# Masked attention with a rational FFN on one core: 64-row score products, sums in PSUM, loads on one queue, a new order

## The chip, the core and the metric

The kernel runs on one core of a Trainium2 chip. The metric is device time in microseconds, the median of several runs. Before the change it is 1323.82 us (three runs, 1321.93 to 1325.02).

## The reference

```python
def _attn_ref(q, k, v, tau):                      # q, k, v: 8 x 8 heads x 576 x 64, f32
    scores = matmul(q, k^T) / sqrt(64)
    thresh = max(scores, axis=-1) - tau
    scores = where(scores >= thresh, scores, -1e9)
    attn = exp(scores - max(scores))
    attn = attn / (sum(attn) + 1e-9)
    return matmul(attn, v)

def _moe_ref(x, w_in, w_out, a, b):               # x: 4608 x 512; w_in 512 x 2048; w_out 2048 x 512
    h = x @ w_in
    P = a[0] + a[1]*h + a[2]*h**2 + a[3]*h**3
    Q = 1 + |b[0]|*|h| + |b[1]|*h**2
    return (P / (Q + 1e-6)) @ w_out
```

The attention's output, heads side by side, is the x of the second function. Only scores within tau of their row's maximum survive.

## The kernel before

**Attention units.** The 64 heads are worked in 32 pairs, `bp`, four pairs to each of 8 batches. A head pair's queries lie in one buffer `QQ`, head 0 in partitions 0 to 63 and head 1 in 64 to 127 (the contracted dimension is 64); its keys lie likewise in `KK`. There are two buffers of each (`NQ = 2`). A pair has four *full* units, 128 queries of both heads, and one *rest* unit, the last 64 queries (`REM`) of both heads put on 128 PSUM partitions: 160 units in all. A unit makes 128 x 576 scores per head (one such tile for a rest unit).

One unit goes through these steps (functions in `unit_ops`):

- `f_qk` (L760 for rest units, L769 and L773 for full ones): the score products on TensorE. A full unit has two 64-row products of 512 keys, one per head, and one 128-row product for the last 64 keys of both, with zeros laid in `KK` so that the heads don't mix. A rest unit has two 128-row products, again with zeros in `QQ`. They write three PSUM banks, 0 to 2 (or 3 to 5, taken in turns, in the first 21 units, `SINGLE`). Head 0 lies at the start of bank 0 and runs 64 columns into bank 1; head 1 ends at the end of bank 2 and begins in the last 64 columns of bank 1. The middle of bank 1 is unused.
- `f_max` (L779, L781) on VectorE, then `f_thr` (L786, L788) on either of ScalarE and VectorE.
- `f_pre` (L794) on ScalarE reads the scores from PSUM and leaves the masked ones in an SBUF buffer `e`; after it the banks are free for the next unit.
- `f_sum` (L798) on ScalarE: the exponential, in place in `e`, with its row sum written by the accumulator (a second instruction, ACTIVATION_READ_ACCUMULATOR) to a small SBUF tile `st`.
- `f_rec`, `f_rec2` (L803 or L805, L809): one over the sum.
- `f_hi`, `f_lo` (L303, L305, L820): the weights as two f16 parts; `f_tp` (L830): two DMA transposes from SyncE's queue; `f_av` (L889): the products with v, as column-split products on halves of the array; `f_xh`, `f_xl` (L899, L905): the result as two f16 parts, the FFN's x. In the first batch the transposes are products with a diagonal matrix instead (L843, L848, L873).

**FFN steps** (`moe_ops`): groups of four 128-row slices of the hidden layer for 256 tokens: `f_g1` (L1006, 128-row f16 products), `f_h` (L1015), the rational function on VectorE and ScalarE (L1020 to L1048), a split in two parts (L295, L297, L1056) and `f_g2` (L1065, f32r products). Weights are decoded from f64 words at the start. The last three token chunks are left for the time after the attention.

**Loads.** `load_ops` loads the queries (`ldq`, L614 to L616) and the keys (`ldk`, L621 to L626) of a pair, twice per pair for three of a batch's four pairs, 56 visits in all. Queries take three DMAs, keys three to five. For the first eight pairs they go out on SyncE (keys of the first two pairs on ScalarE's queue), for the others on GpSimd's queue. There they stand with the loads of v, of the weights and with the output stores. A load waits for a free buffer, and everything behind it on its queue waits with it.

**What sets the order.** Each of these steps is entered with `op(engine, duration, key, ...)` in a planner, `Plan`. It goes through all steps, gives each engine whichever of its ready steps can start first by the planner's durations (ties within `TOL` go to the smaller key), assigns banks and buffers, and calls the steps' functions in the order of planned starts. That order is the program's; at run time each engine goes through its own list in order, with semaphores between. Steps that can run on either of two engines (`FLEX`) are weighed by `EARLY` and `PRICE`. Where TensorE would idle before 400 us, filler products are put in (`f_warm`, L1205). `plan.rank` is the unit's place, which also sets who gets buffers first.

Of the kernel before, what the change touches and what calls it, by code (L numbers as in the profile page):

```python
# [8 lines left out]
F32 = mybir.dt.float32  # L9
# [28 lines left out]
SINGLE = 21  # L38
# [7 lines left out]
NQ = 2  # L46
# [15 lines left out]
UP = 2.0 ** -14  # L62
TPD = 1.3

AHEAD_RANK = 2.3359
# [9 lines left out]
        "ev": {"ACT": 0.465, "DVE": 0.6}, "ev1": {"ACT": 0.156, "DVE": 0.196}, "A": {"ACT": 0.583, "DVE": 0.341},  # L75
        "gh": {"ACT": 0.52, "DVE": 0.33}, "wh": {"ACT": 0.57, "DVE": 0.38}}

EARLY = {"ACT": 1.2758, "DVE": 3.4372}
EARLY_END = 714.5248
PRICE = {"ACT": 1.064, "DVE": 2.2723}  # L80

TOL = {"PE": 0, "ACT": 0.129, "DVE": 0.1, "POOL": 0.1, "DMA": 0, "GD": 0}
WARM, WARM_END = 0.6, 400.0
# [24 lines left out]
class Plan:  # L108
# [7 lines left out]
    def __init__(self):  # L116
        self.ops, self.pools = [], {}
        self.warm = None
        self.banks = [0.0] * 8
        self.rank = 0.0  # L120

    def pool(self, name, n):
        self.pools[name] = [(0.0, i) for i in range(n)]
# [1 line left out]
    def op(self, eng, dur, key, fn, after=(), take=(), drop=()):  # L125
        engs = {eng: dur} if isinstance(eng, str) else eng
        o = Op(engs, key, fn, [x for x in after if x is not None], list(take), list(drop))
        o.rank = self.rank
        self.ops.append(o)
        return o  # L130

# [122 lines left out]
def masked_attention_rational_ffn(  # L254
# [83 lines left out]
    ones = bass.AP(one.tensor, one.offset, [list(one.ap[0]), [0, P]])  # L338


    QW = S + REM
    QQs = [const.tile([P, QW], F32, name=f"QQ{i}") for i in range(NQ)]
    KKs = [const.tile([P, QW + REM], F32, name=f"KK{i}") for i in range(NQ)]
    for t in QQs:
        nc.gpsimd.memset(t[:, NT * P:], 0.0)
    for t in KKs:
        nc.gpsimd.memset(t[0:D, S:QW], 0.0)
        nc.gpsimd.memset(t[D:P, 0:REM], 0.0)
# [40 lines left out]
    def scale_ops(key, get, up, inv, s, after, ahead=0.0):  # L389


        box = {}
        plan.rank = key - ahead
# [12 lines left out]
        def f_all():  # L406
            box["all"] = bank(hb)[:, 0:P]
            nc.tensor.matmul(box["all"], ones, box["d"], start=True, stop=True)

        def f3():  # L410
            p2 = box["p2"]
            nc.vector.tensor_reduce(box["m2"], box["all"], AX.X, ALU.max)
# [32 lines left out]
    def decode_ops(i, key, load, hold, dst=None):  # L445


        box = {}
        plan.rank = key - AHEAD_RANK
        ht = Hold("u", 1)  # L450

        def ld():
            if not loaded:

                for x in KKs[0][:, REM:REM + 1], QQs[0][:, 0:1]:
# [146 lines left out]
    def load_ops(bp, ts):  # L602
        bb, pr = divmod(bp, NP)
        p = pos[(bp, ts[0])]
        plan.rank = p - 3.0
# [4 lines left out]
        queue, eng = (nc.sync, "DMA") if bp < EARLY_BP else (nc.gpsimd, "GD")  # L610

        def ldq():
            QQ = QQs[qh.slot]
            queue.dma_start(QQ[0:D, 0:S], qT[bb, pr, :, 0:S])  # L614
            queue.dma_start(QQ[D:P, 0:NT * P], qT[bb, pr, :, S + REM:])
            queue.dma_start(QQ[D:P, S:], qT[bb, pr, :, S:S + REM])  # L616

        def ldk():
            KK = KKs[kh.slot]
            kq_ = nc.scalar if bp < FROM_ACT else queue  # L620
            kq_.dma_start(KK[0:D, REM:S], kT[bb, pr, :, 0:NT * P])  # L621
            kq_.dma_start(KK[D:P, REM:QW], kT[bb, pr, :, S + REM:])
            kq_.dma_start(KK[0:D, 0:REM], kT[bb, pr, :, NT * P:S])
            if NT in ts:
                for i in range(2):
                    kq_.dma_start(KK[i * D:(i + 1) * D, QW:], kT[bb, pr, :, NT * P + i * REM:S + i * REM])  # L626

        q_done[bp] = [op(eng, 4.3 if first else 1.6, p0, ldq, (), [qh])]
        k_done[bp] = [op(eng, 0.1 if bp < FROM_ACT else 1.6, p0 + 0.1, ldk, (), [kh])]

    def is_plain(bp, t):

# [10 lines left out]

    def load_v_ops(bp):
        bb, pr = divmod(bp, NP)
        plan.rank = pos[(bb * NP, 0)]
# [79 lines left out]

    def unit_ops(bp, t):
        bb, pr = divmod(bp, NP)
        plan.rank = p = pos[(bp, t)]
        full = t < NT  # L730
        single = units.index((bp, t)) < SINGLE
        heads = (0, 1) if full else (0,)
        kh, qh = kq[bp]
        plain = is_plain(bp, t)
# [15 lines left out]
        def f_qk():  # L750
            QQ, KK = QQs[qh.slot], KKs[kh.slot]
            h = sh[0]
            s = ps[:, h.bank[0]:h.bank[-1] + 1, :].rearrange("p b k -> p (b k)")
            w = len(h.bank) * 512
            one = dict(start=True, stop=True)
            if not full:

                s = box["s"][0] = s[:, 0:S]
                for k0, c0, n in (REM, 0, NT * P), (QW, NT * P, REM):
                    nc.tensor.matmul(s[:, c0:c0 + n], QQ[:, NT * P:QW], KK[:, k0:k0 + n], **one)  # L760
                return

            box["s"][0], box["s"][1] = s[:, 0:S], s[:, w - S:]
            box["both"] = bass.AP(s.tensor, s.offset, [list(s.ap[0]), [w - S, 2], [1, S]])
            for hh in range(2):

                r = slice(hh * D, (hh + 1) * D)
                d = s[:, 0:NT * P] if hh == 0 else s[:, w - NT * P:]
                nc.tensor.matmul(d, QQ[r, t * P:(t + 1) * P], KK[r, REM:S], **one)  # L769

            dst, src = (bass.AP(x.tensor, x.offset, [list(x.ap[0]), [n, 2], [1, REM]])
                        for x, n in ((s[:, NT * P:S], w - 2 * NT * P - REM), (KK[:, 0:REM], S)))
            nc.tensor.matmul(dst, QQ[:, t * P:(t + 1) * P], src, **one)  # L773
# [16 lines left out]
        def f_pre(hh):  # L790
# [2 lines left out]
                box["e"] = place(e_hold)  # L793
            nc.scalar.activation(ev(hh), box["s"][hh], AF.Prelu, scale=SCALE, bias=box["st"][:, 2 + hh:3 + hh], alpha=STEEP)  # L794

        def f_sum(hh):
            e = box["e"][:, hh * S:(hh + 1) * S]
            nc.scalar.activation(e, e, AF.Exp, scale=passes, accum_out=box["st"][:, 4 + hh:5 + hh])  # L798

        def f_rec():  # L800
            r = box["st"][:, 6:6 + nh]
            if plan.eng == "ACT":
                nc.scalar.activation(r, box["st"][:, 4:4 + nh], AF.Copy, scale=UP, bias=1e-9 * UP)  # L803
            else:
                nc.vector.tensor_scalar(r, box["st"][:, 4:4 + nh], 1e-9, UP, ALU.add, ALU.mult)  # L805

        def f_rec2():
            r = box["st"][:, 6:6 + nh]
# [103 lines left out]
        qk = op("PE", 1.47 if full else 1.12, p, f_qk, need, [sh[0]], [kh, qh] * nh)  # L912
        if full:
            mx = op("DVE", 1.255, p + 0.1, lambda: f_max(None), [qk], [st_hold])
        else:
# [3 lines left out]
            ex[hh] = op("ACT", 0.63, p + 0.2 + 0.02 * hh, lambda hh=hh: f_pre(hh),  # L919
                        [thr[hh]] + ([ex[0]] if hh else []), [e_hold] if hh == 0 else (), [sh[hh]])  # L920
        for hh in heads:
            mk[hh] = op("ACT", 0.76, p + 0.3 + 0.02 * hh, lambda hh=hh: f_sum(hh), [ex[hh]])
# [51 lines left out]
    def moe_ops(ck, f0, nb, p, begins, ends, soon):  # L974
# [2 lines left out]
        kind, bb, half = ck  # L977
        late = p >= end
        g = f0 // NC
        plan.rank = p = max(p, w_key(g, 2 * NC) - 1.0, ranks[-1] + 0.01)  # L980
        ranks.append(p)
        name = f"{kind}{bb}_{half}_{f0}"
        FW = nb * CT
# [264 lines left out]
```

## Time and profile before

| | before |
|---|---|
| median of three runs | 1323.82 us (1321.93 to 1325.02) |
| span of the profiled execution | 1321.7 us |
| its granted TensorE clock, mean | 0.987 |
| TensorE busy | 1258.0 us (95%) |
| VectorE busy | 1218.1 us (92%) |
| ScalarE busy | 1118.6 us (85%) |
| GpSimd busy | 241.0 us (18%) |
| DMA moved | 146.67 MB, mean 111 GB/s |

The span, from first to last instruction of the profiled execution, is the only time given of that execution; it is 2.1 us under the median of the runs. In the rows PE is TensorE's products, PEld its weight loads, DVE VectorE, ACT ScalarE, POOL GpSimd, SP SyncE; a letter q behind an engine means its queue. A group's row gives line, engine, operation, operands, shapes and count, then total busy time and mean ns of one, then the idle time of the engine just before these instructions and what ended it. Ends of products are modelled, so lengths of single products overlap their successors, and starts are the safer reading.

### The profile page before, as it was taken

Reading aid. Unit: us, or ns where it says so; the run is one execution under the profiler, and the core shown is the slowest. Engines: PE = TensorE matmul, PEld = TensorE weight load, DVE = VectorE, ACT = ScalarE, POOL = GpSimd, SP = SyncE. Lnnn points to the kernel's source line nnn. Section 1 sums busy time; section 2 is a strip of 40 time slices with the busy share of each in tenths; the row PEclk is TensorE's granted clock in tenths of the full one; section 3 lists DMA queues with packets and bytes.
Section 4 is the critical chain, followed back from the end, with each engine's and each line's share of the span. In section 5 each row is a group of like instructions: output and inputs, shape, how many; then the busy total and the mean of one; then the engine's idle time right before and its main releaser. Section 6 shows DMA issues by size and latency. Waiting matters only on the chain. (4 is left out here: it accounts for less than half of the span.)

```text
span 1321.7 us, 25463 instructions
## 1 busy us (share of the span) xinstructions
PE 1258.0 (95%) x9476; PEld 936.0 (71%) x9476; DVE 1218.1 (92%) x1913; ACT 1118.6 (85%) x2182; POOL 241.0 (18%) x462
## 2 busy tenths in 40 slices
PE   7987998999999999999999899998999999999998
PEld 5665776777777767676677677766677777678886
DVE  4988999999999999998999899988999999998777
ACT  4998888899999989998999789877988899885564
POOL 2101000022312321322212231223212330200000
PEclk8999999999999999999999999999999999999999
DMA  7434373576767756665665584586765864641000
GB/s 203 130 101 140 106 152 73 99 137 129 144 115 119 150 104 121 118 138 117 117 97 105 94 155 102 126 116 118 127 104 108 144 146 81 134 82 37 17 17 16
DMA packets 340588, 146.67 MB, mean 111 GB/s; under 512 B 316208, under 2 KB 323184, under 8 KB 340464
## 3 DMA queue, kind: packets, MB, share of 16 engines
q1 hardware_dynamic: 316400, 86.49, 38.4%
q0 software_dynamic: 22784, 57.31, 15.9%
q10 hardware_dynamic: 1280, 1.25, 0.4%
q8 instruction: 75, 1.23, 0.4%
q14 instruction: 49, 0.40, 0.1%
HBM read 60.30 MB, written 9.44 MB: 53 GB/s over the span
## 5 line engine op out<-in xcount | busy, mean ns | idle before, releaser
L1065 PE MATMUL banks<-wp,g 128*128 128x512 f32 x1728 | 438.9, 403 | 3.9 <-DVE g L1056 3.0
L1006 PEld LDWEIGHTS <-wi 128*128 128x128 f16 x3456 | 332.7, 98 | 71.6 <-issue 33.5
L1006 PE MATMUL banks<-x,wi 128*128 128x256 f16 x3072 | 361.3, 274 | 14.5 <-ACT t L1015 13.3
L1065 PEld LDWEIGHTS banks<-wp,g 128*128 128x128 f32 x1728 | 315.3, 189 | 77.5 <-DVE g L1056 5.8
L798 ACT ACTIVATE e<-e,cf 128x576 f32<-128x576 f32 x288 | 221.5, 775 | 0.3
L303 ACT ACTIVATE hi<-e,st 128x576 f16<-128x576 f32 x229 | 174.0, 768 | 51.9 <-DVE st L809 40.1
L794 ACT ACTIVATE e<-banks,st 128x576 f32<-128x576 f32 x288 | 205.1, 735 | 11.0 <-DMA KK<-in_kT_dram 6.0
L820 DVE SCALAR_TENSOR_TENSOR e<-e,st,hi 128x576 f16<-128x576 f32 x252 | 204.1, 810 | 9.0 <-ACT hi L303 7.2
L779 DVE TENSOR_REDUCE st<-banks 128x2 f32<-128x1152 f32 x128 | 172.1, 1344 | 14.2 <-PE banks L773 13.9
L769 PE MATMUL banks<-KK,QQ 64*128 64x512 f32 x512 | 154.8, 652 | 9.1 <-DMA KK<-in_kT_dram 5.3
L889 PE MATMUL banks<-pT,V 128*64 128x256 f16 (+1 forms) x2520 | 125.2, 253 | 14.0 <-DMA pT<-e 9.3
L889 PEld LDWEIGHTS <-V 128*64 128x64 f16 x2520 | 107.4, 113 | 33.3 <-issue 24.2
L1015 ACT ACTIVATE t<-banks,hsc 128x512 f32<-128x512 f32 (+1 forms) x192 | 106.2, 575 | 24.2 <-PE banks L1006 19.0
L1042 DVE SCALAR_TENSOR_TENSOR t<-t,co,t 128x1024 f32<-128x1024 f32 (+1 forms) x73 | 92.1, 1262 | 18.9 <-ACT t L1036 18.9
L773 PEld LDWEIGHTS banks<-KK,QQ 128*128 128x128 f32 x256 | 38.6, 190 | 99.3 <-issue 88.7
L1033 ACT ACTIVATE t<-t,co 128x1024 f32<-128x1024 f32 (+1 forms) x73 | 82.7, 1133 | 29.8 <-DVE t L1039 29.3
L614 POOL DMA_DIRECT2D QQ<-in_qT_dram x42 | 22.1, 527 | 413.8 <-PE banks L760 248.0
L1056 DVE TENSOR_TENSOR g<-t,g 128x512 fp32r<-128x512 f32 x144 | 94.5, 682 | 2.6 <-ACT g L295 2.5
L1048 DVE SCALAR_TENSOR_TENSOR t<-t,co,t 128x1024 f32<-128x1024 f32 (+1 forms) x73 | 92.2, 1263 | 0.8
L1026 DVE SCALAR_TENSOR_TENSOR t<-t,co 128x1024 f32<-128x1024 f32 (+1 forms) x73 | 92.0, 1261 | 0.4 <-ACT t L1015 0.4
L1039 DVE SCALAR_TENSOR_TENSOR t<-t,co,t 128x1024 f32<-128x1024 f32 (+1 forms) x73 | 92.0, 1260 | 0.0
L1029 DVE SCALAR_TENSOR_TENSOR t<-t,co 128x1024 f32<-128x1024 f32 (+1 forms) x73 | 92.0, 1260 | 0.0
(130 smaller groups left out, 1540.7 us busy)
## 6 DMA issues: line engine op xcount, KB each, us to landing
t<-in_w_in_dram POOLq DMA_DIRECT2D x16, 512.0 KB, 5.1
t<-in_w_out_dram POOLq DMA_DIRECT2D x16, 512.0 KB, 4.9
out_dram<-u POOLq DMA_DIRECT2D x26, 256.0 KB, 3.0
V<-in_v_dram POOLq DMA_DIRECT2D x24, 256.0 KB, 4.6
QQ<-in_qT_dram POOLq DMA_DIRECT2D x42, 144.0 KB, 2.8
KK<-in_kT_dram POOLq DMA_DIRECT2D x42, 144.0 KB, 3.3
QQ<-in_qT_dram POOLq DMA_DIRECT2D x42, 128.0 KB, 2.7
KK<-in_kT_dram POOLq DMA_DIRECT2D x42, 128.0 KB, 2.7
```

The lines of the kernel that those rows point to most:

```text
L303: nc.scalar.activation(dst, src, AF.Identity, scale=factor)
L769: nc.tensor.matmul(d, QQ[r, t * P:(t + 1) * P], KK[r, REM:S], **one)
L779: nc.vector.tensor_reduce(box["st"][:, 0:2], box["both"], AX.X, ALU.max, negate=True)
L794: nc.scalar.activation(ev(hh), box["s"][hh], AF.Prelu, scale=SCALE, bias=box["st"][:, 2 + hh:3 + hh], alpha=STEEP)
L798: nc.scalar.activation(e, e, AF.Exp, scale=passes, accum_out=box["st"][:, 4 + hh:5 + hh])
L820: nc.vector.scalar_tensor_tensor(box["lo"][:, c], ev(hh), box["st"][:, 6 + hh:7 + hh], box["hi"][:, c], ALU.mult, ALU.subtract)
L889: nc.tensor.matmul(dst, V[:, c * P + hh * D:c * P + (hh + 1) * D], rhs, start=c == 0 and n == 0, stop=c == NT and n == 2)
L1006: nc.tensor.matmul(d, wi_tile(c, f0 + j, hl), x[:, c, :], start=c == 0 and n == 0, stop=c == NC - 1 and n == 2)
L1015: nc.scalar.activation(box["h3"][:, 2 * k:2 * k + 2, sl], psv[:, :, sl], AF.Identity, scale=hsc[:, b2, g:g + 1])
L1048: nc.vector.scalar_tensor_tensor(box["r"], box["r"], a0, box["q"], ALU.add, ALU.mult)
L1056: nc.vector.tensor_tensor(fr(g[:, 1]), box["r"][:, k * GW:(k + 1) * GW], g[:, 0], ALU.subtract)
L1065: nc.tensor.matmul(acc[tt], fr(g[:, x]), fr(wo[f][y]), start=begins and j == n == 0, stop=ends and j == nb - 1 and n == 2)
```

## The change

- **Scores.** `f_qk` uses 64-row products alone. A full unit has four, in this order: head 0's last 64 keys (bank 1), head 1's first 512, head 0's first 512, head 1's last 64 (bank 1). The two that write bank 1 use different halves of the array, and a `nop` on TensorE with a manual dependency (`ORDERED`) stands between, so that the fourth is issued after the first is done. A rest unit has four 64x64 products, each head on a quarter of the array. The zeros in `QQ` and `KK` go, and so do the memsets that made them.
- **Sums.** In units after the first 21, `f_sum` writes its row sums to unused columns of bank 1 (eight places in turn) in place of `st`, and `f_rec` reads them there.
- **Loads.** Queries and keys are one DMA each. All go out on SyncE's queue, but the keys of the first two pairs, which stay on ScalarE's.
- **Order.** `EARLY` and `PRICE` have new values. Each call of `plan.begin` (a unit, a load, a weight piece, an FFN step) gets an offset from a table `TURN`, added to its steps' keys and to its rank; each kind of step gets one from a table `KIND`, added to the key. The planner's durations for the score products go from 1.47 to 1.25 and from 1.12 to 1.15, for an exponential from 0.76 to 0.72, for loads from 1.6 to 0.9.

The diff, cut to its core (the tables have 366 and 67 entries):

```diff
+ORDERED = mybir.DependencyInfo(mybir.DependencyClass.Sync, mybir.DependencyReason.DATA)
...
-EARLY = {"ACT": 1.2758, "DVE": 3.4372}
+EARLY = {"ACT": 1.8676, "DVE": 3.6438}
-PRICE = {"ACT": 1.064, "DVE": 2.2723}
+PRICE = {"ACT": 1.2025, "DVE": 2.8579}
+TURN = [
+    11048, -2112, 3481, -19656, -6304, 1054, -1453, 497, -1076, -1197, -290, -766, 442, -75, 84, 564, -1390, 1586,
...
+KIND = [
+    9993, 10627, -7782, -183, -77, 427, -553, 632, -567, -291, -802, -8543, -1609, -2589, 86, -17567, 588, -7123,
...
-        o.rank = self.rank
+        o.turn, o.kind = self.turn, self.kinds.setdefault(fn.__code__, len(self.kinds))
+        turn = TURN[o.turn] / 1000 if o.turn < len(TURN) else 0.0
+        o.key += turn
+        o.key += KIND[o.kind] / 1000 if o.kind < len(KIND) else 0.0
+        o.rank = self.rank + turn
...
-            queue.dma_start(QQ[0:D, 0:S], qT[bb, pr, :, 0:S])
-            queue.dma_start(QQ[D:P, 0:NT * P], qT[bb, pr, :, S + REM:])
-            queue.dma_start(QQ[D:P, S:], qT[bb, pr, :, S:S + REM])
+            nc.sync.dma_start(QQs[qh.slot][:, :], qT[bb, pr].rearrange("d (h s) -> h d s", h=2))
...
+            kq_ = nc.scalar if bp < FROM_ACT else nc.sync
+            kq_.dma_start(KKs[kh.slot][:, :], kT[bb, pr, :, 0:2 * S].rearrange("d (h s) -> h d s", h=2))
...
-                for k0, c0, n in (REM, 0, NT * P), (QW, NT * P, REM):
-                    nc.tensor.matmul(s[:, c0:c0 + n], QQ[:, NT * P:QW], KK[:, k0:k0 + n], **one)
+                for c0, n, k in (NT * P, REM, (NT * P, 0)), (0, NT * P, (0, REM)):
+                    for hh in range(2):
+                        r = slice(hh * D, (hh + 1) * D)
+                        q0 = (NT * P, 0)[hh]
+                        nc.tensor.matmul(s[r, c0:c0 + n], QQ[r, q0:q0 + REM], KK[r, k[hh]:k[hh] + n], **one)
...
-            for hh in range(2):
+            for hh, k0, n, d0 in (0, NT * P, REM, NT * P), (1, REM, NT * P, w - NT * P), (0, 0, NT * P, 0), (1, 0, REM, w - S):
                 r = slice(hh * D, (hh + 1) * D)
-                d = s[:, 0:NT * P] if hh == 0 else s[:, w - NT * P:]
-                nc.tensor.matmul(d, QQ[r, t * P:(t + 1) * P], KK[r, REM:S], **one)
...
-            nc.tensor.matmul(dst, QQ[:, t * P:(t + 1) * P], src, **one)
+                if d0 == w - S:
+                    tc.add_manual_dep(nc.tensor.nop().ins, shared.ins.name, ORDERED, reason="one bank")
+                mm = nc.tensor.matmul(s[:, d0:d0 + n], QQ[r, hh * REM + t * P:hh * REM + (t + 1) * P], KK[r, k0:k0 + n], **one)
+                if d0 == NT * P:
+                    shared = mm
...
+        def total(h0, h1):
+            if single:
+                return box["st"][:, 4 + h0:4 + h1]
+            o = S - 512 + 2 * (place_of[bp, t] % 8)
+            return ps[:, 1, o + h0:o + h1]
...
-            nc.scalar.activation(e, e, AF.Exp, scale=passes, accum_out=box["st"][:, 4 + hh:5 + hh])
+            nc.scalar.activation(e, e, AF.Exp, scale=passes, accum_out=total(hh, hh + 1))
```

More of the change, by code (lines that the diff above doesn't have):

```diff
@@ L119, in __init__, with begin @@
         self.banks = [0.0] * 8
-        self.rank = 0.0
+        self.rank, self.turn, self.kinds = 0.0, 0, {}
+    def begin(self, rank):
+        self.rank, self.turn = rank, self.turn + 1
+        return rank
     def pool(self, name, n):
@@ L338, in masked_attention_rational_ffn @@
     ones = bass.AP(one.tensor, one.offset, [list(one.ap[0]), [0, P]])
[L341 to L348, printed above, removed]
+    QQs = [const.tile([P, S], F32, name=f"QQ{i}") for i in range(NQ)]
+    KKs = [const.tile([P, S], F32, name=f"KK{i}") for i in range(NQ)]
     nc.vector.tensor_scalar(passes, cf[:, 6:7], 0.0, None, ALU.is_ge)
@@ L392, in scale_ops @@
         box = {}
-        plan.rank = key - ahead
+        plan.begin(key - ahead)
         h, hd, hb = Hold("sc", 1), Hold("u", 1), Hold("b", 1, B1)
@@ L448, in decode_ops @@
         box = {}
-        plan.rank = key - AHEAD_RANK
+        plan.begin(key - AHEAD_RANK)
         ht = Hold("u", 1)
@@ L453, in ld @@
             if not loaded:
-                for x in KKs[0][:, REM:REM + 1], QQs[0][:, 0:1]:
+                for x in KKs[0][:, 0:1], QQs[0][:, 0:1]:
                     nc.gpsimd.tensor_scalar(cf[:, 15:16], x, 1.0, 1.0, ALU.mult, ALU.mult)
@@ L604, in load_ops @@
         p = pos[(bp, ts[0])]
-        plan.rank = p - 3.0
+        plan.begin(p - 3.0)
         n = sum(2 if t < NT else 1 for t in ts)
@@ L609, in load_ops @@
         p0 = p - (4.6 if first else 4.0)
-        queue, eng = (nc.sync, "DMA") if bp < EARLY_BP else (nc.gpsimd, "GD")
         def ldq():
-            QQ = QQs[qh.slot]
-            queue.dma_start(QQ[0:D, 0:S], qT[bb, pr, :, 0:S])
-            queue.dma_start(QQ[D:P, 0:NT * P], qT[bb, pr, :, S + REM:])
-            queue.dma_start(QQ[D:P, S:], qT[bb, pr, :, S:S + REM])
+            nc.sync.dma_start(QQs[qh.slot][:, :], qT[bb, pr].rearrange("d (h s) -> h d s", h=2))
         def ldk():
[L619 to L629, printed above, removed]
+            kq_ = nc.scalar if bp < FROM_ACT else nc.sync
+            kq_.dma_start(KKs[kh.slot][:, :], kT[bb, pr, :, 0:2 * S].rearrange("d (h s) -> h d s", h=2))
+        q_done[bp] = [op("DMA", 2.8 if first else 0.9, p0, ldq, (), [qh])]
+        k_done[bp] = [op("DMA", 0.1 if bp < FROM_ACT else 0.9, p0 + 0.1, ldk, (), [kh])]
+    place_of = {u: i for i, u in enumerate(units)}
     def is_plain(bp, t):
@@ L645, in load_v_ops @@
         bb, pr = divmod(bp, NP)
-        plan.rank = pos[(bb * NP, 0)]
+        plan.begin(pos[(bb * NP, 0)])
         vhold = vh_[bp] = Hold("v", NT // 2 + 1)
@@ L728, in unit_ops @@
         bb, pr = divmod(bp, NP)
-        plan.rank = p = pos[(bp, t)]
+        p = plan.begin(pos[(bp, t)])
         full = t < NT
-        single = units.index((bp, t)) < SINGLE
+        single = place_of[bp, t] < SINGLE
         heads = (0, 1) if full else (0,)
@@ L764, in f_qk @@
             box["both"] = bass.AP(s.tensor, s.offset, [list(s.ap[0]), [w - S, 2], [1, S]])
-            for hh in range(2):
+            for hh, k0, n, d0 in (0, NT * P, REM, NT * P), (1, REM, NT * P, w - NT * P), (0, 0, NT * P, 0), (1, 0, REM, w - S):
                 r = slice(hh * D, (hh + 1) * D)
-                d = s[:, 0:NT * P] if hh == 0 else s[:, w - NT * P:]
[L769 to L773, printed above, removed]
+                if d0 == w - S:
[3 more added lines that the diff above has]
+                    shared = mm
         def f_max(hh):
@@ L802, in f_rec @@
             if plan.eng == "ACT":
-                nc.scalar.activation(r, box["st"][:, 4:4 + nh], AF.Copy, scale=UP, bias=1e-9 * UP)
+                nc.scalar.activation(r, total(0, nh), AF.Copy, scale=UP, bias=1e-9 * UP)
             else:
-                nc.vector.tensor_scalar(r, box["st"][:, 4:4 + nh], 1e-9, UP, ALU.add, ALU.mult)
+                nc.vector.tensor_scalar(r, total(0, nh), 1e-9, UP, ALU.add, ALU.mult)
         def f_rec2():
@@ L911, in unit_ops @@
         need = k_done[bp] + q_done[bp]
-        qk = op("PE", 1.47 if full else 1.12, p, f_qk, need, [sh[0]], [kh, qh] * nh)
+        qk = op("PE", 1.25 if full else 1.15, p, f_qk, need, [sh[0]], [kh, qh] * nh)
         if full:
@@ L921, in unit_ops @@
         for hh in heads:
-            mk[hh] = op("ACT", 0.76, p + 0.3 + 0.02 * hh, lambda hh=hh: f_sum(hh), [ex[hh]])
+            mk[hh] = op("ACT", 0.72, p + 0.3 + 0.02 * hh, lambda hh=hh: f_sum(hh), [ex[hh]])
         rec = op(FLEX["rec"], 0, p + 0.4, f_rec, list(mk.values()))
@@ L979, in moe_ops @@
         g = f0 // NC
-        plan.rank = p = max(p, w_key(g, 2 * NC) - 1.0, ranks[-1] + 0.01)
+        p = plan.begin(max(p, w_key(g, 2 * NC) - 1.0, ranks[-1] + 0.01))
         ranks.append(p)
```

22 rows, old and new, of tables (KIND, TURN) are left out of this document.

## The prediction

> **What bounds the kernel now.** I read the engine totals on the page first, then busy time by stage, then the groups by line, then the timeline around single score tiles. The page's totals:
>
> ```profile
> span 1321.7 us, 25463 instructions
> PE 1258.0 (95%) x9476; PEld 936.0 (71%) x9476; DVE 1218.1 (92%) x1913; ACT 1118.6 (85%) x2182; POOL 241.0 (18%) x462
> ```
>
> Busy time in four stages (start; two halves of the steady part; the FFN tail):
>
> ```profile
> 0.00:250.00 250.00, 222.22 (x1571) 164.73 (x1572) 217.00 (x442) 207.44 (x440) 22.44 (x58) 0.96 0.48 126
> 250.00:715.00 465.00, 452.82 (x3526) 332.40 (x3523) 444.90 (x662) 428.69 (x840) 109.12 (x202) 1.00 0.64 123
> 715.00:1180.00 465.00, 446.35 (x3440) 326.56 (x3438) 441.46 (x686) 401.60 (x775) 108.28 (x200) 0.99 0.63 116
> 1180.00:1321.00 141.00, 136.65 (x950) 112.29 (x946) 114.73 (x128) 80.89 (x130) 1.13 (x2) 1.00 0.11 27
> ```
>
> The columns are length, then busy time of PE, PEld, DVE, ACT, POOL, granted clock, DMA. In the steady 930 us PE stands 30.9 us, DVE 43.6, ACT 99.7: PE and DVE bound it together, ACT has a tenth to spare, POOL nothing to do with it. In the first 250 us PE stands 27.8 us, and part of its busy time is filler (the L1205 row below, 36.4 us, issued only where PE would wait). So all that a better order could ever take from PE is about 63.7 (1321.7 - 1258.0) + 36.4 = 100 us, two thirds of it in the start.
>
> **The score products (PE).** By form, matmul rows, the last two being full 128-column products:
>
> ```profile
> L769 PE MATMUL banks<-KK,QQ 64*128 64x512 f32 x512 | 154.8, 652 | 9.1 <-DMA KK<-in_kT_dram 5.3 <-ACT e L794 3.7
> L773 PE MATMUL banks<-KK,QQ 128*128 128x128 f32 x256 | 63.3, 329 | 0.0
> ...
> L843 PE MATMUL banks<-u,e 128*128 128x128 f32 x288 | 37.7, 280 | 5.5 <-DVE u L836 2.8 <-ACT pT L295 1.9 <-DVE sc L412 0.7
> L1205 PE MATMUL banks<-ident 128*128 128x128 f32 x244 | 36.4, 304 | 1.4 <-POOL ident masks.py:199 1.4
> ...
> L760 PE MATMUL banks<-KK,QQ 128*128 128x64 f32 x64 | 10.6, 247 | 0.0
> ```
>
> and the weight loads of two tiles in time (start, length), then of a tile that column-split work follows:
>
> ```profile
> 1175.48 0.30 PEld L769 LDWEIGHTS banks<-KK,QQ 64*128 64x128 f32 x4 [0.36 <-ACT e L798]
> 1176.54 0.30 PEld L773 LDWEIGHTS banks<-KK,QQ 128*128 128x128 f32 x2 [0.76 <-issue]
> 1176.76 1.24 PEld L1065 LDWEIGHTS banks<-wp,g 128*128 128x128 f32 x6
> ...
> 1183.14 0.30 PEld L760 LDWEIGHTS banks<-KK,QQ 128*128 128x128 f32 x2
> ...
> 1184.16 2.83 PEld L1006 LDWEIGHTS <-wi 128*128 128x128 f16 x26
> ```
>
> ```profile
> 605.26 0.30 PEld L773 LDWEIGHTS banks<-KK,QQ 128*128 128x128 f32 x2 [0.76 <-issue]
> 605.68 0.36 PEld L889 LDWEIGHTS <-V 128*64 128x64 f16 x8
> ```
>
> Every f32 product is two instructions. The two 64-row products of a full tile run side by side on the two halves of the array: four of 512 columns, and L773's load comes 1.06 us after theirs (1176.54 - 1175.48), which is one load (0.11: two loads span 0.30, one lasts 0.19), two instructions of 0.43, and 0.10 in which the array empties before the split changes. L773 then takes 0.22 if 128-row work follows (1176.76 - 1176.54) and 0.42 if column-split work does (605.68 - 605.26, once more emptying). A full tile is now 1.28 or 1.48 from load to next load.
>
> After: each half has a 64-column and a 512-column product. 64 columns are not half of 128: L760's 64-column row is 10.6/64 = 0.166 an instruction, L843's 128-column row 37.7/288 = 0.131. The loads of 128 weights, 0.11 apart, pace both. So 0.11 + 2 x 0.11 + 2 x 0.43 + 0.10 = 1.29 (rounded 1.27 to 1.29), and the emptying now comes after every tile. Against 1.28 that is nothing; against 1.48, about -0.2. If a sixth of the 128 tiles (an estimate) have column-split work behind them: -4 us. Lower bound: the small products cost columns alone (half of 0.131, so 0.13 for two in place of L773's 0.42 with its emptying) and the emptying behind the tile costs nothing more: 1.48 less 0.42 and plus 0.13 is 1.19, against the 1.28 and 1.48 of now at most -0.22 a tile, -28, which is also what the durations in the diff book (1.47 to 1.25). Upper bound: the two small products don't overlap and each adds L760's 2 x 0.166: +0.12 a tile, +15. I take -4, since L760 is the nearest row.
>
> The Trainium skill, page "TensorEngine Tiling (Array Packing)", section "Instruction Overhead", says that a product has about 60 cycles of overhead, below which width is free. By it 64 columns would cost little more than their columns, and the full tiles would give some 13 us (an estimate); L760's 0.166 against L843's 0.131 says otherwise here.
>
> The 64-query tile: L760 has no split and needs 1.02 (1184.16 - 1183.14) with nothing emptying. As 64x64 products of two heads it splits the array, so it pays emptying before and after and shows its successor's load: a load of half the weights, so 0.06, then 0.11 + 0.86 + 0.10 = 1.13, plus 0.1 + 0.1, less 1.02: +0.3 x 32 = +10. Lower bound the table's +0.03 (+1 us); upper bound no overlap of the heads, another 0.9 each (+29). L769 shows that halves do overlap: I take +7. PE in sum +3.
>
> The new PE wait (a nop that holds the fourth product until the first is done) holds everything behind it on PE. The first is over 0.3 us into the tile; the cover is 0.86 us of 512-column work already issued. Cost 0; without that cover 0.3 x 128 = +38.
>
> **The sums (ACT).**
>
> ```profile
> L798 ACT ACTIVATE e<-e,cf 128x576 f32<-128x576 f32 x288 | 221.5, 775 | 0.3
> L794 ACT ACTIVATE e<-banks,st 128x576 f32<-128x576 f32 x288 | 205.1, 735 | 11.0 <-DMA KK<-in_kT_dram 6.0 <-DMA pT<-e 3.0 <-issue 0.3
> L779 DVE TENSOR_REDUCE st<-banks 128x2 f32<-128x1152 f32 x128 | 172.1, 1344 | 14.2 <-PE banks L773 13.9
> ...
> L798 ACT ACTIVATION_READ_ACCUMULATOR e<-e,cf 128x1 f32 x288 | 57.3, 199 | 0.0
> ...
> L786 ACT ACTIVATE st<-st,cf 128x2 f32<-128x2 f32 x91 | 26.2, 288 | 22.3 <-DVE st L779 21.9
> ```
>
> No row writes a sum to PSUM. The nearest is L794, the same shape with a PSUM operand, 40 ns shorter than L798. Of the 199 ns, 0 to -40 can go, in the tiles after the 21st (some 250 sums): 0 to -10 us of ACT. ACT isn't the bound: -1.
>
> The sums now lie in bank 1, into which the next tile's products, its maximum (L779) and its first exponentials go too. One tile in time:
>
> ```profile
> 811.80 1.34 ACT L794 ACTIVATE e<-banks,st 128x576 f32<-128x576 f32 x2
> ...
> 813.04 0.77 ACT L798 ACTIVATE e<-e,cf 128x576 f32<-128x576 f32 x1
> ...
> 813.73 1.13 PE L769 MATMUL banks<-KK,QQ 64*128 64x512 f32 x4
> 813.80 0.77 ACT L798 ACTIVATE e<-e,cf 128x576 f32<-128x576 f32 x1
> ...
> 814.46 0.20 ACT L798 ACTIVATION_READ_ACCUMULATOR e<-e,cf 128x1 f32 x1
> 814.69 0.20 ACT L803 ACTIVATE st<-st 128x2 f32<-128x2 f32 x1
> ```
>
> The next tile's products (813.73) run beside the second sum (813.80) and the reader of both (814.69). If the bank is one user's at a time, this can't be: either products wait for the sums, 0.9 us later (814.66), or the sum waits for the products, and all of ACT behind it, some 1.4 us. Does the loop bear it? A tile's chain is products 1.48 + L779 1.34 + L786 0.29 + L794 1.34 + four hand-offs taken at 0.25 (an estimate; PE's stop on ACT at 1175.48 is 0.36) = 5.5 us; sums (813.04 to 814.66 = 1.6) and L803 0.2 make it 7.3. The 128 full and 32 half tiles fill 1180 us, 8.2 a full tile. It fits, with 0.9 us left. Likeliest +4; bounds 0 and the first rival.
>
> The Trainium skill, "PSUM — Partial Sum Buffer", section "PSUM bank collisions raise a hardware error", says just this: two engines on one bank and quadrant collide whichever columns they touch, and software must keep them apart. No row here has two engines in one bank, so none tests it.
>
> **Loads.** POOL loses three query and two key DMAs for each of 42 visits, and 90 small key ones, 300 in all at about 0.53 us, 159 of its 241 us. SP gets two for each of these visits, 84, and of its own loads two or more a visit go.
>
> ```profile
> L614 POOL DMA_DIRECT2D QQ<-in_qT_dram x42 | 22.1, 527 | 413.8 <-PE banks L760 248.0 <-PE banks L773 163.3 <-PE banks L1065 2.5
> ```
>
> ```profile
> SPq L614 <- PE banks L760: 66.5, 5, 26.9
> ```
>
> ```profile
> pT<-hi SPq DMA_TRANSPOSE x140, 3.4
> pT<-e SPq DMA_TRANSPOSE x140, 3.3
> ...
> KK<-in_kT_dram POOLq DMA_DIRECT2D x90, 16.0 KB, 3.8
> ```
>
> ```profile
> 813.26 1.28 SPq L830 DMA_TRANSPOSE pT<-e  x1
> ```
>
> SP has 280 transposes x 1.28 = 358 us and then about 60 us of loads in 1180: room enough. But the waits for a free buffer (413.8 us on POOL, where V loads and output stores queued behind them) move to SP, where the transposes queue behind them. In the order they stand where the buffer comes free: 0, the third rival otherwise. The start gains something definite:
>
> ```profile
> 2.93 0.61 SPq L616 DMA_DIRECT2D QQ<-in_qT_dram  x1
> ...
> 7.92 1.13 PE L769 MATMUL banks<-KK,QQ 64*128 64x512 f32 x4
> ...
> 18.27 3.34 PE L769 MATMUL banks<-KK,QQ 64*128 64x512 f32 x4 [5.31 <-DMA KK<-in_kT_dram]
> ```
>
> Two of the first three issues and the memsets ahead of them go: the first product comes about 1.5 us earlier, and of the 5.3 us stop at 18.27 part goes: -3 (0 to -7).
>
> **The order.** It has no price of its own; its bounds are the 100 us above and, on the other side, the rivals. DVE, untouched, allows less: 43.6 us idle in the steady part. I take a third of start's 64 (-19) and a quarter of the steady 31 (-8): -27.
>
> **Sum.** The span of 1321.7 lies 2.1 under the median 1323.8; against the median: +3 - 1 + 4 + 0 - 3 - 27 = -24, 1300 us. Likeliest case, chance 0.45, its own range 1284 to 1318.
>
> **Rivals.**
> 1. Slower: the bank. In every tile whose products stand between the two sums in program order, ACT stands 1.4 us; ACT has 99.7 us to spare in the steady part, about 0.8 a tile. If half of the 139 tiles do so that is 97 us, and if two thirds of it passes to the end, +65, less the 24 gained: about 1365; with a third passing, 1332. Middle 1345. It decides from about 35 tiles. For: the row at 813.73. Against: the chain fits. Chance 0.25.
> 2. Faster still: small products cost only columns, -28 in place of -4: about 1276. Against: L760's 0.166. For: the table's 1.25. Chance 0.16.
> 3. SP's waits hold up transposes: 13 us a wait (66.5/5); if ten of 54 visits hold a pair by 5 us beyond its slack, +50 less 24: 1350. Chance 0.06.
> 4. The change brings nothing: PE's work per tile stays and DVE's 95% closes the rest, 1323. Chance 0.08.
>
> Faster by over 0.2% (about what a measurement of this kernel can tell): 0.45 + 0.16, and the easy end of the first rival, 0.02: 0.63. Within: 0.08. Slower: 0.29. The range runs from a little under the second rival to the middle of the first: 1268 to 1347.
>
> **What would show it.** Right: L769-like products with next load 1.27 us on, whatever follows; PE's busy time near 1258, not 1230; the accumulator read near 160 ns; filler under 36 us. Wrong: ACT waiting on PE before L798 (first rival), a score group under 1.2 us (second), SP's transposes late behind loads (third). The forecast fails if the bank's waits outweigh the gain in order, the least certain term.

## The result, and the profile after

The changed kernel takes 1803.26 us (median of four runs, 1802.12 to 1809.68) against 1324.42 (four runs of the kernel before beside them, 1321.93 to 1332.05): a ratio of 1.361, 95% interval 1.356 to 1.366. The forecast was 1300, range 1268 to 1347. The profiled execution's span is 1807.9 us, its granted clock 0.875.

From the page of the changed kernel, the totals and two of its rows of forty slices, busy tenths of PE and granted clock:

```profile
span 1807.9 us, 26061 instructions
...
PE 1343.8 (74%) x9836; PEld 1016.5 (56%) x9836; DVE 1226.6 (68%) x1907; ACT 1130.5 (63%) x2192; POOL 83.6 (5%) x156
...
PE   3699688777777658696677755967667757877998
...
PEclk6899899889888789798798868988789878988999
```

Busy time by stage (length, then busy PE, PEld, DVE, ACT, POOL, clock, DMA share, GB/s):

```profile
0.00:250.00 250.00, 175.57 (x1310) 136.35 (x1311) 173.58 (x390) 170.39 (x376) 21.67 (x52) 0.88 0.43 111
250.00:715.00 465.00, 352.72 (x2605) 263.51 (x2605) 323.83 (x477) 302.53 (x575) 20.62 (x34) 0.88 0.68 84
715.00:1180.00 465.00, 332.61 (x2415) 248.93 (x2413) 303.29 (x442) 282.29 (x557) 21.17 (x36) 0.85 0.65 76
1180.00:1665.00 485.00, 346.80 (x2590) 256.87 (x2589) 312.15 (x473) 293.37 (x551) 19.06 (x32) 0.85 0.62 80
1665.00:1807.00 142.00, 136.06 (x923) 110.80 (x921) 113.71 (x131) 81.95 (x135) 1.08 (x2) 1.00 0.14 31
```

The FFN tail, the last 142 us, is what it was (141 us, PE 136.65 busy). All of the loss lies in the stages with attention. From 250 to 1665 us PE now stands 383 of 1415 us, 27 in a hundred, where it stood 3 in a hundred of its steady stages, and no other engine is full either: DVE and ACT have their old work (1226.6 and 1130.5 us) in a longer time. When no engine is full, the time is in waits. The longest on PE, ACT and DVE, in the view of waits (us in total, times, longest; GpSimd's waits for free buffers, which stand above them there, are left out, for GpSimd is off the chain):

```profile
...
DVE st L837 <- ACT st L831: 197.7, 71, 15.0
...
ACT e L826 <- PE banks L793: 173.5, 56, 15.1
PEld banks L793 <- ACT e L826: 152.8, 63, 12.7
...
PE banks L793 <- DMA KK<-in_kT_dram: 144.8, 14, 23.1
PE banks L793 <- ACT e L826: 130.8, 50, 12.4
...
PE banks L917 <- DMA pT<-e: 74.2, 20, 11.9
ACT e L816 <- DMA pT<-e: 73.5, 12, 8.4
```

Two things stand side by side: waits on transfers (keys, `KK`, 10 us each in the mean and up to 23; transposes, `pT`, 4 to 6 in the mean and, in these rows, up to 12), and score products (L793) and exponentials (L826) that wait for each other. (L831 and L837 are the two steps of one over the sum, which come next.) In a chain like this one wait is passed on to the next engine, so the list alone can't divide the loss; the experiments do. What each looks like in the timeline:

*The transfers.* The start, then one load late in the run:

```profile
0.78 1.12 ACTq L645 DMA_DIRECT2D KK<-in_kT_dram  x1
...
1.21 0.71 SPq L641 DMA_DIRECT2D QQ<-in_qT_dram  x1
...
14.20 0.18 POOL L486 TENSOR_SCALAR cf<-KK 128x1 f32<-128x1 f32 x1 [12.29 <-DMA KK<-in_kT_dram]
...
16.74 4.01 PE L793 MATMUL banks<-KK,QQ 64*128 64x64 f32 x13 [9.42 <-DMA QQ<-in_qT_dram]
```

```profile
1469.34 0.53 SPq L641 DMA_DIRECT2D QQ<-in_qT_dram  x1
1469.92 0.51 SPq L645 DMA_DIRECT2D KK<-in_kT_dram  x1
...
1471.44 9.41 SPq L858 DMA_TRANSPOSE pT<-hi  x1
...
1480.96 3.03 SPq L858 DMA_TRANSPOSE pT<-e  x1
...
1484.00 2.47 PE L793 MATMUL banks<-KK,QQ 64*128 64x64 f32 x8 [9.85 <-DMA KK<-in_kT_dram]
```

With little else to move, keys issued at 0.78 are there at 14.20, when the GpSimd instruction that reads them (L486) can start, and the first product comes at 16.74 where it came at 7.92. The keys issued at 1469.92 take 14 us again, to 1484.00, and the transpose behind them on SyncE, an issue of 1.28 us before, is held for 9.41. Counted in the trace's packet records, each load is 128 packets of 2304 bytes (14336 in 112 loads) of 100 ns, and in 84% of the 727 us in which any of them moves exactly two move at once: 128 x 0.1 / 2 = 6.4 us a load. A second load adds no third packet (three move in 6% of the time), so the two of a visit take 13. Before, pieces of a load of half the size landed in about 3 us:

```profile
QQ<-in_qT_dram POOLq DMA_DIRECT2D x42, 144.0 KB, 2.8
KK<-in_kT_dram POOLq DMA_DIRECT2D x42, 144.0 KB, 3.3
```

*The bank.* The first sum of one unit, the products of the next, and the second exponential of the first unit, in the middle of the run:

```profile
912.58 0.15 ACT L826 ACTIVATION_READ_ACCUMULATOR e<-e,cf 128x1 f32 x1
912.90 0.73 PEld L793 LDWEIGHTS banks<-KK,QQ 64*128 64x128 f32 x7 [0.36 <-ACT e L826]
912.90 1.35 PE L793 MATMUL banks<-KK,QQ 64*128 64x64 f32 x8
...
914.18 3.33 PEld L1093 LDWEIGHTS banks<-wp,g 128*128 128x128 f32 x15
...
914.36 0.78 ACT L826 ACTIVATE e<-e,cf 128x576 f32<-128x576 f32 x1 [1.63 <-PE banks L793]
```

The products wait for the first sum (0.36), run, and the second exponential starts only after them: ScalarE stands 1.63 us. Before, the two ran side by side. Both waits are semaphore waits of the program (ScalarE's is the instruction ahead of its exponential, at 914.30), though sums and products write different columns of the bank. What would come of it without them was not tried.

### The profile page after: what moved, and what is told of

Same layout as the page of the kernel before. It is cut to its first block, busy times and chain, and to the rows that moved or that the text cites. A ratio compares the mean times of both kernels' runs of the same rounds, so it can differ in the third digit from the quotient of the medians.

```text
span 1807.9 us, 26061 instructions
## 1 busy us (share of the span) xinstructions
PE 1343.8 (74%) x9836; PEld 1016.5 (56%) x9836; DVE 1226.6 (68%) x1907; ACT 1130.5 (63%) x2192; POOL 83.6 (5%) x156
## 3 DMA queue, kind: packets, MB, share of 16 engines
q8 instruction: 78, 1.28, 0.3%
## 5 line engine op out<-in xcount | busy, mean ns | idle before, releaser
L1093 PE MATMUL banks<-wp,g 128*128 128x512 f32 x1728 | 461.6, 416 | 8.5 <-DVE g L1084 5.5
L793 PE MATMUL banks<-KK,QQ 64*128 64x512 f32 (+1 forms) x1024 | 207.8, 526 | 288.7 <-DMA KK<-in_kT_dram 144.8
L1034 PEld LDWEIGHTS <-wi 128*128 128x128 f16 x3456 | 338.5, 101 | 107.6 <-issue 56.1
L1034 PE MATMUL banks<-x,wi 128*128 128x256 f16 x3072 | 384.9, 284 | 17.7 <-ACT t L1043 13.1
L1093 PEld LDWEIGHTS banks<-wp,g 128*128 128x128 f32 x1728 | 325.4, 196 | 105.5 <-issue 14.4
L793 PEld LDWEIGHTS banks<-KK,QQ 64*128 64x128 f32 x1024 | 136.6, 219 | 373.3 <-issue 195.1
L826 ACT ACTIVATE e<-e,cf 128x576 f32<-128x576 f32 x288 | 223.5, 777 | 194.3 <-PE banks L793 173.5
L816 ACT ACTIVATE e<-banks,st 128x576 f32<-128x576 f32 x288 | 207.1, 738 | 88.6 <-DMA pT<-e 73.5
L917 PE MATMUL banks<-pT,V 128*64 128x256 f16 (+1 forms) x2520 | 147.0, 275 | 108.8 <-DMA pT<-e 74.2
L339 ACT ACTIVATE hi<-e,st 128x576 f16<-128x576 f32 x221 | 168.3, 771 | 70.6 <-DMA pT<-hi 38.2
L917 PEld LDWEIGHTS <-V 128*64 128x64 f16 x2520 | 122.5, 123 | 135.8 <-issue 95.0
L837 DVE RECIPROCAL st<-st 128x2 f32<-128x2 f32 (+1 forms) x160 | 25.8, 161 | 198.3 <-ACT st L831 197.7
```

Of the source, the lines that this page charges most:

```text
L339: nc.scalar.activation(dst, src, AF.Identity, scale=factor)
L793: mm = nc.tensor.matmul(s[:, d0:d0 + n], QQ[r, hh * REM + t * P:hh * REM + (t + 1) * P], KK[r, k0:k0 + n], **one)
L826: nc.scalar.activation(e, e, AF.Exp, scale=passes, accum_out=total(hh, hh + 1))
L917: nc.tensor.matmul(dst, V[:, c * P + hh * D:c * P + (hh + 1) * D], rhs, start=c == 0 and n == 0, stop=c == NT and n == 2)
L1034: nc.tensor.matmul(d, wi_tile(c, f0 + j, hl), x[:, c, :], start=c == 0 and n == 0, stop=c == NC - 1 and n == 2)
L1093: nc.tensor.matmul(acc[tt], fr(g[:, x]), fr(wo[f][y]), start=begins and j == n == 0, stop=ends and j == nb - 1 and n == 2)
```

## The experiments

**Undoing one thing each.** The first is the changed kernel with queries and keys laid in memory as 128 rows of 576 numbers (both heads), so that the transfer's outermost dimension is 128 and not 2:

```diff
-            nc.sync.dma_start(QQs[qh.slot][:, :], qT[bb, pr].rearrange("d (h s) -> h d s", h=2))
+            nc.sync.dma_start(QQs[qh.slot][:, :], qT[bb, pr])
...
-            kq_.dma_start(KKs[kh.slot][:, :], kT[bb, pr, :, 0:2 * S].rearrange("d (h s) -> h d s", h=2))
+            kq_.dma_start(KKs[kh.slot][:, :], kT[bb, pr])
```

> The changed kernel with one edit: queries and keys lie in memory as 128 rows of 576, so each load is still one transfer from SyncE, but its outermost dimension is 128 rows on both sides and not two heads. Order, products and sums as changed. Theory A (a transfer with an outermost dimension of 2 runs on few DMA engines, takes 14 us instead of 3, and holds up the transposes behind it): the time falls by most of the 480 us, to 1350 to 1450, loads take 3 to 5 us, and what is left above 1324 is the bank's. Theory B (the shared bank 1 is the cause, the loads are late because everything is): 1750 to 1803.

The second puts the sums back to SBUF:

```diff
-            if single:
-                return box["st"][:, 4 + h0:4 + h1]
-            o = S - 512 + 2 * (place_of[bp, t] % 8)
-            return ps[:, 1, o + h0:o + h1]
+            return box["st"][:, 4 + h0:4 + h1]
```

> The changed kernel with one edit: the sums go to the small SBUF tile again in all units; loads, products and order as changed. Theory A: 1650 to 1780, the loads still take 14 us. Theory B: 1320 to 1400; ScalarE's waits of its exponentials on TensorE (173.5 us in the changed kernel) go and take the rest with them.

The third does both:

> Both edits at once: loads as 128 rows, sums in SBUF. What is left of the change is the 64-row products, SyncE for all loads and the new order. If loads and bank are the whole loss, this is at or under the kernel before: 1290 to 1325, 1300 by the terms of my prediction without the bank's. If the new order or the 64-row products cost time themselves, it stays over 1340.

The fourth is the kernel before with one thing of the change, the sums of the units after the first 21 in bank 1:

> The kernel before with one part of the change: sums of the units after the first 21 in the middle of bank 1, read there; its own order, loads and products. If sums and products of neighbouring units shut each other out of the bank, 1345 to 1400 with ScalarE's second sum waiting about 1.5 us for TensorE in many units. If the bank costs nothing, 1315 to 1324 (40 ns less for each of some 250 sums, mostly hidden).

Measured (median, range; ratio to before with 95% interval):

| | us | ratio |
|---|---|---|
| 128-row loads | 1399.33 (1398.43 to 1400.93) | 1.057 [1.053, 1.061] |
| sums in SBUF | 1743.24 (1739.66 to 1745.89) | 1.317 [1.312, 1.321] |
| both | 1278.04 (1274.56 to 1280.05) | 0.965 [0.962, 0.969] |
| before, sums in bank 1 | 1382.15 (1377.67 to 1386.84) | 1.044 [1.040, 1.049] |

The load's shape is worth 404 us with the sums in bank 1 (1803 to 1399) and 465 with them in SBUF (1743 to 1278). The bank is worth 121 us in the new order (1278 to 1399), 59 in the old (1324 to 1382), 60 beside the slow loads. With both undone the change is a gain of 3.5%, a little more than the 1290 to 1325 that was expected of it: this is the fastest version of the study. Its DMA issues (KB each, us from issue to landing), from the page:

```profile
QQ<-in_qT_dram SPq DMA_DIRECT2D x56, 288.0 KB, 3.0
KK<-in_kT_dram SPq DMA_DIRECT2D x52, 288.0 KB, 3.7
...
pT<-hi SPq DMA_TRANSPOSE x140, 3.3
pT<-e SPq DMA_TRANSPOSE x140, 3.3
```

From the same queue, queries land 3.0 and keys 3.7 us after their issue, where keys behind queries took 14, and the same 14336 packets are on the move for 152 us in place of 727, in 61% of it 10 to 17 at a time. Here are the two steady stages of this version, for comparison with the 30.8 us in 930 (the forecast's 30.9) that PE stood before: it stands 15.2 us in 880.

```profile
250.00:715.00 465.00, 456.82 (x3728) 349.23 (x3728) 456.94 (x685) 425.77 (x844) 33.23 (x56) 1.00 0.60 123
715.00:1130.00 415.00, 407.99 (x3371) 311.62 (x3370) 406.10 (x621) 381.10 (x729) 26.04 (x44) 1.00 0.58 120
```

In the version with 128-row loads and sums in bank 1, the waits that are left are the bank's:

```profile
PEld banks L793 <- ACT e L826: 90.5, 84, 2.4
ACT e L826 <- PE banks L793: 81.5, 55, 2.8
DVE st L837 <- ACT st L831: 62.3, 69, 2.6
PE banks L793 <- ACT e L826: 61.5, 70, 2.0
...
ACT st L831 <- PE banks L793: 43.0, 36, 2.9
```

81.5 us in 55 waits is 1.48 us a unit, and PE and DVE wait in turn. With sums in SBUF no exponential waits for score products and no product (row PE) waits for an exponential; the 5.2 us that L793 still waits on `e` are for L816, which reads the scores out of the banks.

**Outermost dimension or memory layout?** The 128-row version changes both. This one keeps the changed kernel's layout and volume, has sums in SBUF, and splits each load by head:

```diff
-            nc.sync.dma_start(QQs[qh.slot][:, :], qT[bb, pr].rearrange("d (h s) -> h d s", h=2))
+            for h in range(2):
+                nc.sync.dma_start(QQs[qh.slot][h * D:(h + 1) * D, :], qT[bb, pr, :, h * S:(h + 1) * S])
```

(and the keys in the same way.)

> The changed kernel with sums in SBUF and each load of queries or keys as two transfers, one per head, each with 64 rows as its outermost dimension; the memory layout stays that of the changed kernel. If an outermost dimension of two is what makes the transfer run two pieces at a time, this gives 1270 to 1290, like the 128-row version, with transfers of some 3 us. If the strided rows in memory, or the volume of the rows read twice, is the cause, it stays above 1600.

1293.63 us (1291.11 to 1295.20; 0.977 [0.973, 0.981]): 450 of the 465 us come back. Twice the number of transfers, each with 64 rows outermost, and the same strided rows in memory. So it is the outermost dimension of the transfer; the layout in memory is not to blame. (The changed load's pattern has three dimensions and these have two; that the size 2 and not the third dimension sets the time rests on the two packets at a time.) The 4 us over the expectation, 16 over the version with one transfer, go with 108 more transfers on SyncE: PE's waits on keys are 13.6 us here, 4.8 there.

**Is it the queue that they stand in?** The version with sums in SBUF and two-piece loads, but the loads of all pairs after the eighth on GpSimd's queue, away from the transposes (the keys go to `queue` too):

```diff
+        queue = nc.sync if bp < 8 else nc.gpsimd
...
-            nc.sync.dma_start(QQs[qh.slot][:, :], qT[bb, pr].rearrange("d (h s) -> h d s", h=2))
+            queue.dma_start(QQs[qh.slot][:, :], qT[bb, pr].rearrange("d (h s) -> h d s", h=2))
...
-            kq_ = nc.scalar if bp < FROM_ACT else nc.sync
+            kq_ = nc.scalar if bp < FROM_ACT else queue
```

> The changed kernel with sums in SBUF and its own two-piece loads, but with the loads of all but the first eight pairs issued by GpSimd's queue, so that no transpose stands behind them on their queue. If the transposes are late because they stand behind the slow transfers on SyncE's queue, most of the 465 us come back: 1290 to 1400. If the slow transfers hold up the transposes on the DMA engines that they occupy, or if the score products wait for the loads themselves, it stays above 1500.

1575.79 us (1574.02 to 1581.09; 1.190 [1.184, 1.196]): above 1500, as expected if the transfers do harm on any queue; still 167 of 465 us come back, so the queue has a part. From its page and, below it, its waits and some transposes:

```profile
QQ<-in_qT_dram POOLq DMA_DIRECT2D x42, 288.0 KB, 9.7
KK<-in_kT_dram POOLq DMA_DIRECT2D x42, 288.0 KB, 10.7
```

```profile
PE banks L795 <- DMA KK<-in_kT_dram: 111.3, 12, 23.1
...
ACT hi L339 <- DMA pT<-hi: 56.7, 16, 10.9
```

```profile
796.71 6.98 SPq L857 DMA_TRANSPOSE pT<-e  x1
803.78 6.39 SPq L857 DMA_TRANSPOSE pT<-hi  x1
810.27 1.33 SPq L857 DMA_TRANSPOSE pT<-e  x1
```

The loads are late on any queue, and a transpose can still be held (6.98 and 6.39 us for 1.28) with no load before it in its queue in this stretch. The packets of the two loads that GpSimd issued at 791.59 and 793.51 move from 793 to 810 us, but for two us between them: the issues are long while the loads move and short (1.33) when they are done. The run changes more than the place in the queue, though. Of the time in which packets of these 84 loads move, two move at once in 40% and four in 43%, so that here queries and keys can move side by side, and they land in 10 us and not 14. The 167 us, about a third, are thus the worth of the other queue, and standing behind the load is only a part of it. How the rest divides between late keys and transposes held while the loads move was not tried; the first eight pairs are still on SyncE in this run.

**Sharing the bank, or PSUM as such?** Sums in PSUM once more, on top of the fastest version, but in bank 7, which no other work then uses; and its control with bank 7 empty.

```diff
-B2, B3, BA, B1, BH = [(0, 1, 2), (3, 4, 5)], [(0, 1, 2)], [(3,), (4,), (5,)], [(7,), (6,), (5,)], [(5,), (6,)]
+B2, B3, BA, B1, BH = [(0, 1, 2), (3, 4, 5)], [(0, 1, 2)], [(3,), (4,), (5,)], [(6,), (5,)], [(5,), (6,)]
...
-            return ps[:, 1, o + h0:o + h1]
+            return ps[:, 7, o + h0:o + h1]
```

> The version with 128-row loads and the new order, with sums in PSUM again for the units after the first 21, but in bank 7, which is taken from all other work (the v products and fillers use the other banks). If the 121 us that sums in bank 1 cost come from sharing the bank with the next unit's score products, this is within 8 us of its control without sums in bank 7, perhaps some us faster, by the accumulator read of 160 for 199 ns (288 times 39 ns is 11 us of ScalarE). If reading and writing the sums in PSUM costs it, wherever they lie, it is 100 us or more above the control.

> The control for the sums in bank 7: the same version with bank 7 taken from all work and left unused, sums in SBUF. It gives the price of one bank fewer: 1278 if the bank is not missed, up to 1320 if the v products wait for banks.

1361.48 us (1360.53 to 1364.08) with the sums in bank 7, 1360.22 (1356.39 to 1361.91) with it empty: 1.3 us, within their ranges. The 121 us are the sharing, not the write or the read, as far as a plan with seven banks can show it. The accumulator read into PSUM is 34 to 40 ns shorter (161 ns with sums in bank 1, the row below, of the version with 128-row loads; 167 in bank 7; 201 in SBUF) and buys nothing here:

```profile
L826 ACT ACTIVATION_READ_ACCUMULATOR e<-e,cf 128x1 f32 x288 | 46.5, 161 | 0.0
```

The control itself missed: one bank fewer costs 82 us, not 0 to 42.

**Where the gain of 46 us comes from.** Four versions without the load's shape and without sums in PSUM. The new planner (tables, prices, durations) alone, on before's products and loads:

> Before, with the changed kernel's planner (its turns, kinds, early starts, prices and durations) and nothing else of the change: before's products, before's load pieces on their old queues, sums in SBUF. It prices the order alone. If the order is what makes the version with 128-row loads and SBUF sums 45 us faster than before, this gives 1280 to 1295. If the gain lies in the products or in the loads' queue, it stays at 1318 to 1328. My forecast had -27 for the order and -3 for the start, which would be about 1294.

Before's order with the new products, and 128-row loads on the queues of before:

> Before's order, with the changed kernel's 64-row score products, and queries and keys in one transfer each of 128 rows by 576 columns, on the queues that before uses; sums in SBUF. It prices products and the smaller number of loads without SyncE. The forecast's product term is +3 and it had nothing for fewer transfers: 1320 to 1330. If the shared-row products of before cost more than their columns, as the rival on the small products has it, about 1300. If the gain of the 128-row version lies here, about 1280.

The same with all loads on SyncE:

> The kernel with before's order and 64-row products, with all of its loads of queries and keys issued by SyncE rather than by GpSimd's queue. It prices the queue. If loads on SyncE cost nothing, as the forecast took it, it is within 5 us of the same kernel with the old queues. If a load's wait for its buffer holds up the transposes behind it, it is 20 to 40 us slower than that, with VectorE or TensorE waiting on transposes in the chain of waits.

New planner, new products, loads on the old queues:

> The version with 128-row loads, sums in SBUF and the new order, with the loads of all but the first eight pairs put back on GpSimd's queue. The order alone on before's products cost 7 us; with the new products and SyncE's loads it gains some 30. If the order needs the new products, whose durations it is planned with, this gives 1275 to 1290. If it needs the loads on SyncE, where they don't wait behind stores and v, 1310 to 1330.

| order | products, loads | loads' queue | us | ratio |
|---|---|---|---|---|
| new | old | old | 1331.27 (1324.88 to 1344.61) | 1.007 [1.003, 1.010] |
| old | new | old | 1316.50 (1311.14 to 1320.75) | 0.994 [0.992, 0.997] |
| old | new | SyncE | 1307.64 (1305.36 to 1309.98) | 0.988 [0.984, 0.992] |
| new | new | old | 1295.81 (1291.64 to 1305.25) | 0.979 [0.973, 0.986] |
| new | new | SyncE | 1278.04 (1274.56 to 1280.05) | 0.965 [0.962, 0.969] |

Step by step from before: products and fewer transfers -7, SyncE -9, order -30; then, to the changed kernel, bank +121 and load shape +404. The steps are not independent: the order costs 7 us on the old products and loads, for whose durations it isn't planned, and gives 21 on the new ones with the old queues; SyncE gives 9 in the old order and 18 in the new. Runs of one version in this table lie up to 20 us apart, so steps of this size are good to a few us. The expectations missed four times here. The order alone was to give 1294. Products and fewer transfers gave more than the 1320 to 1330 expected. SyncE was to change nothing or cost 20 to 40. The new order with the old queues falls between its two cases, 1275 to 1290 and 1310 to 1330, so it needs the products and gains from SyncE as well. Whether on the old products it is their durations or their many small loads that spoil the order was not tried apart.

The rest tile in the version with the old order and old queues, and the next load:

```profile
1176.10 0.31 PEld L748 LDWEIGHTS banks<-KK,QQ 64*64 64x64 f32 x8 [0.21 <-ACT e L785]
...
1177.22 5.79 PEld L993 LDWEIGHTS <-wi 128*128 128x128 f16 x54 [0.81 <-issue]
```

SyncE's own waits for free buffers in the fastest version:

```profile
SPq L641 <- PE banks L783: 109.1, 23, 26.2
SPq L641 <- PE banks L793: 84.3, 21, 18.1
```

## Why the prediction was wrong, step by step

- **The step that failed: Loads, taken as 0.** The forecast counted issues and waits on the queues and never asked how the transfer itself runs; the one landing that it showed was that of an old, small load (16 KB, 3.8 us). Measured: two pieces at a time, 13 to 14 us for the two loads of a visit, +404 us with the sums in bank 1 and +465 with them in SBUF. The queue, the other half of this term, was no cost but a gain of 9 to 18. The row that would have warned is not in the profile of before; it is in the diff, `"d (h s) -> h d s"`, which puts a dimension of 2 outermost. The Trainium skill, page "DMA: Bandwidth & Descriptors", section "Why a DMA increments its semaphore by 16 and not by 1", says that the number of DMA engines of a transfer is the largest up to 16 that divides the size of the slowest dimension (other than 1) on both sides. By it the changed load gets two, the one split by head and the 128-row one 16; the packet counts here agree (two at a time, against 10 to 17). I read no rule on this and gave no chance to it.
- **Rival 3 (SyncE holds up the transposes)** got the right victims for the wrong reason. Its priced cause, waits for free buffers, is harmless: in the fastest version SyncE waits 193 us for buffers, and loads on SyncE still gain 9 to 18 us. What holds the transposes is the transfer while it moves, on their queue (9.41 us) and on another (6.98 and 6.39).
- **The bank, +4, with rival 1 at a chance of 0.25.** The mechanism is as rival 1 has it, down to the price: ACT stands 1.4 us forecast, 1.48 to 1.63 measured, in 55 units, where it said half of 139. But it allowed two thirds of that to reach the end, +65; it is +121 in the new order, +59 in the old. It left out that the products wait for the first sum too (61.5 us in 70 waits), and through them PE. The argument "it fits, with 0.9 us left" looked at the loop of a tile and not at PE, which had 3% to spare.
- **The score products, +3.** The full tile is right: weight loads at 905.59 and 906.87, 1.28 us, as 122 of 124 in the fastest version, whatever follows. (Of the forecast's rows of products L843 and L1205 are the full 128-column ones; L760, the last, has 64 columns.)

```profile
905.59 0.73 PEld L793 LDWEIGHTS banks<-KK,QQ 64*128 64x128 f32 x7 [0.36 <-ACT hi L339]
...
906.87 1.21 PEld L1034 LDWEIGHTS <-wi 128*128 128x128 f16 x12
```

  Of 127 tiles in before's trace 16 take 1.4 to 1.6 us, an eighth where the estimate had a sixth; after the new products none does (in the version with the old order). Tiles up to 1.6 us have means of 1.31 and 1.28, which is -4 in 128, as forecast. The rest tile is 1.12 after the change (1176.10 to 1177.22), the 1.13 of the sum without the 0.2 of emptying that I added to it. And the 1.02 taken for it before was among the shortest: the 32 rest tiles of before's trace last 1.02 to 1.22, 1.11 in the mean. So that term is under +1 and not +7, and the products are near -4 and not +3, small beside the rest; the 7 us that products and fewer transfers gave together are not divided further. Rival 2, that small products cost their columns alone, is out: no full tile is at 1.19. Its price was too high as well: by the forecast's own shares of 1.28 and 1.48 (a sixth) a tile of 1.19 saves 0.12, or 16 us, and not 28.
- **The sums on ACT, -1**: right (0, by bank 7). The read is 160 ns, as foreseen.
- **Start, -3**: at 7.42 the first product of the fastest version is 0.5 us earlier, not 1.5, and the stop for keys after it is still 4.8 us and ends at 18.21, where it was 5.3 and ended at 18.27: nothing gained. In the changed kernel the first product is 8.8 us later.
- **Order, -27**: -30 as the last step, +7 as the first. The size came out near for a kernel that has the rest of the change without its two losses, but by luck: it was a guessed third of the start's 64 us and a quarter of the steady stages' 31. In that version PE stands 8 us less in the first 250 us and 16 less in the steady stages, where the forecast had 19 (with filler) and 8. The forecast's 1300 has its counterpart in that version's 1278; most of the difference is SyncE's gain and the products.

## What to carry to other kernels

Read a transfer's access pattern as the hardware gets it: the outermost dimension on both sides has to be large (here 64 or 128, not 2), and one transfer that replaces two can be several times slower than both (here 6.5 us of moving a load, for 1.4 in the 128-row form, by 727 and 152 us for 112 loads). Where a buffer moves into a PSUM bank, list who else writes that bank at that time, on both sides of the wait, and price the wait at the engine that has least to spare. An order tuned to durations can lose with instructions that have others (here +7 for -21 to -30).

## What was not expected

- A load with two pieces in flight also slows others: a transpose behind it was held 9.41 us, for 1.28.
- The clock goes with the gaps: mean granted clock 0.875 in the changed kernel, where PE is busy 74% of the span, 0.985 with 128-row loads (90%), 0.995 with sums in SBUF too (97%). PE's busy time for the same 9836 products is 1343.8, 1254.0 and 1232.4 us, so that waits of PE are in part paid a second time in slower products.
- One PSUM bank of eight is worth 82 us in this kernel (1278 to 1360), more than all that the order gave; how much of it is the other plan that the planner makes with seven banks was not tried.
